# First batch's q and k in two token halves, constant products placed by the plan, and a plan that parts masks from two-input sums

## The chip, the cores and the metric

The kernel runs on one core of a Trainium2 chip. The metric is the device time of one execution in microseconds. The five engines are named as the profile names them: PE (TensorE; PEld are its weight loads), DVE (VectorE), ACT (ScalarE), POOL (GpSimd) and SP (SyncE). Each works through its own list of instructions in order and waits on semaphores for the others.

## What is computed

Attention with a few "beacon" keys in front, followed by a two-layer network. Cut to what matters (q, k and v are 8 batches x 8 heads x 576 tokens x 64, beacon_k and beacon_v have 16 tokens):

```python
k_all = np.concatenate([beacon_k, k], axis=2)          # 592 keys
v_all = np.concatenate([beacon_v, v], axis=2)
scores = scale * np.matmul(q, k_all.transpose(0, 1, 3, 2))
scores = np.where(causal, -1e9, scores)                # beacons are always seen
a = np.exp(scores - scores.max(-1, keepdims=True))
a /= a.sum(-1, keepdims=True) + 1e-09
x = np.matmul(a, v_all)  -> 4608 tokens x 512
h = x @ w_in                                            # 512 x 2048
g = h * (1.0 / (1.0 + np.exp(-1.702 * h)))
out = g @ w_out                                         # 2048 x 512
```

## The kernel before, in words

**Sets and chunks.** Four heads of one batch are a *set*: 128 partitions hold 4 heads x 32 rows. There are 16 sets, two per batch. For each set `e_load_qk` (L400) loads q and k by DMA from POOL's queue (288 KB each as f16, the DMA casts), `e_bk` (L442) casts the beacon keys on DVE and `e_turn` (L449) transposes k and q on DVE in 32x32 blocks (L451 for the beacons, L458 for the rest). A *chunk* is one stretch of score columns: `e_qk` (L477) makes the scores on PE (L491), `e_exp` (L499) takes the exponential on ACT (L502). Masks on the diagonal blocks follow on DVE (L516, a minimum of two inputs; in the first batch where the block lies among the first 288 tokens) or on POOL (L523). `e_av` (L571) multiplies the masked exponentials by ones (the row sums, "ones" in the profile) and by v (L582). DVE turns the sums, takes reciprocals (L592 to L603) and normalizes into xT (L616).

**The first batch.** Its sets 0 and 1 are taken in token halves: the first chunk of each set (qk0, qk1) covers tokens 0 to 287 alone, three more chunks cover the rest (qk2 to qk4 of set 0, qk5 to qk7 of set 1). Each needs the whole of q and k of its set, transposed. The scores of qk1 and qk2 are kept in four single banks of PSUM, those of the others in one large tile s, so that each of these others waits for the exponentials of the one before.

**The network.** Groups of tokens go through `m1` (PE, L640), an activation and `m2` (PE, L685). Later groups use products of fewer multiplications with sums taken by DVE (L705, L754, L770, L841). PSUM's four ring banks u0 to u3 are shared by `av`, `m1`, `m2` and the rest.

**The order.** `ORDER` at the top of the file lists, for each engine, the numbers of the operations in the order in which they are emitted; these lists were written out beforehand. `Plan.run` walks through the lists with a planned duration for each operation, so that every operation has a planned start. From that it does two things: it merges the five lists into one program order, and it gives every ring tile one of the banks, the one that the plan says is free earliest. Instructions of one engine always stand in the order of `ORDER`.

**DMA.** q, k, v, w_in and w_out go through POOL's queue, with at most 8 in flight: POOL waits at the ninth until the first has landed. The beacon keys go through the queues of SP and ACT (`load_bk`, L437), into a buffer that DVE has set to zero before (L305, L306, L1328). Stores of the output use SP.

**Constant products.** `FILL` (L314) names two places at which PE multiplies constants: 72 products of 112 columns ahead of qk0 and 2 products of 256 columns in f32 ahead of qk1 (L1358). No result uses them.

Of the kernel before, what the change touches and what calls it, by code (L numbers as in the profile page):

```python
# [7 lines left out]
F16 = mybir.dt.float16  # L8
# [9 lines left out]
        76, 100, 101, 102, 103, 111, 112, 119, 113, 114, 122, 126, 149, 131, 140, 152, 154, 129, 133, 136, 142, 163,  # L18
        166, 145, 169, 172, 175, 138, 156, 159, 161, 178, 184, 181, 199, 238, 202, 187, 205, 243, 208, 211, 217, 245,
        214, 193, 248, 188, 194, 269, 195, 196, 223, 274, 220, 224, 276, 189, 190, 252, 259, 279, 225, 229, 411, 230,  # L20
        231, 226, 414, 257, 283, 264, 262, 255, 290, 417, 288, 293, 295, 286, 232, 424, 301, 309, 331, 305, 303, 319,
        323, 315, 307, 311, 327, 325, 329, 313, 317, 321, 442, 433, 349, 350, 354, 351, 352, 355, 356, 445, 440, 436,
        438, 357, 360, 471, 370, 371, 361, 376, 377, 577, 365, 362, 363, 378, 366, 580, 481, 372, 367, 373, 368, 586,
        379, 486, 488, 484, 605, 382, 383, 496, 384, 607, 385, 490, 518, 610, 506, 494, 492, 520, 504, 516, 510, 500,
        512, 502, 514, 498, 508, 596, 543, 549, 538, 544, 545, 539, 540, 541, 738, 550, 565, 551, 546, 566, 741, 552,
        599, 603, 601, 619, 744, 554, 555, 556, 557, 624, 626, 622, 751, 559, 560, 561, 562, 567, 769, 634, 571, 572,
        568, 772, 760, 573, 574, 646, 658, 638, 648, 628, 650, 656, 798, 763, 765, 767, 630, 644, 642, 640, 636, 654,
        632, 652, 676, 681, 677, 682, 678, 683, 684, 904, 808, 703, 679, 704, 687, 907, 815, 811, 688, 705, 689, 913,
        692, 690, 697, 706, 698, 932, 699, 693, 694, 695, 700, 934, 813, 923, 709, 710, 711, 937, 712, 835, 817, 829,
        821, 837, 823, 839, 833, 819, 843, 825, 827, 831, 845, 847, 841, 1065, 930, 946, 865, 866, 892, 867, 893,  # L30
        868, 1068, 926, 928, 951, 949, 953, 1071, 894, 876, 877, 895, 878, 1078, 870, 871, 872, 873, 881, 1096, 882,
        883, 879, 884, 886, 1099, 887, 888, 889, 961, 1087, 1125, 898, 899, 900, 901, 967, 977, 957, 969, 959, 963,
        965, 973, 983, 975, 971, 979, 955, 981, 985, 1144, 1135, 1092, 1090, 1030, 1003, 1004, 1005, 1006, 1147,
        1138, 1142, 1140, 1094, 1153, 1008, 1009, 1024, 1014, 1025, 1172, 1010, 1015, 1031, 1011, 1032, 1174, 1026,
        1016, 1019, 1020, 1017, 1177, 1021, 1022, 1027, 1203, 1033, 1209, 1235, 1207, 1036, 1205, 1037, 1211, 1038,
        1212, 1039, 1219, 1215, 1251, 1239, 1163, 1186, 1237, 1241, 1221, 1243, 1223, 1244, 1225, 1247, 1227, 1228,
        1255, 1191, 1170, 1166, 1193, 1168, 1189, 1259, 1257, 1260, 1231, 1288, 1253, 1342, 1289, 1263, 1283, 1326,
        1346, 1284, 1348, 1285, 1344, 1286, 1290, 1350, 1330, 1351, 1294, 1304, 1354, 1295, 1328, 1335, 1358, 1305,
        1332, 1291, 1334, 1296, 1299, 1374, 1338, 1306, 1307, 1297, 1300, 1301, 1302, 1376, 1378, 1380, 1310, 1360,
        1362, 1311, 1312, 1364, 1382, 1383, 1316, 1313, 1367, 1366, 1317, 1386, 1318, 1319, 1449, 1370, 1406, 1407,  # L40
        1453, 1408, 1411, 1481, 1409, 1412, 1455, 1451, 1465, 1413, 1483, 1457, 1414, 1485, 1467, 1469, 1487, 1458,
        1417, 1461, 1427, 1490, 1489, 1418, 1428, 1419, 1420, 1429, 1474, 1471, 1473, 1497, 1422, 1493, 1423, 1430,
        1424, 1425, 1477, 1499, 1503, 1433, 1501, 1434, 1435, 1439, 1440, 1436, 1505, 1534, 1441, 1442, 1509, 1529,
        1530, 1531, 1506, 1540, 1532, 1541, 1535, 1550, 1551, 1536, 1537, 1542, 1545, 1552, 1546, 1547, 1543, 1548,
        1553, 1556, 1557, 1558, 1559, 1562, 1563, 1564, 1565,
    ],
    "ACT": [
        3, 1, 77, 79, 105, 106, 104, 107, 120, 115, 118, 123, 116, 117, 141, 143, 164, 167, 146, 170, 173, 176, 179,
        182, 185, 200, 239, 203, 206, 244, 209, 212, 246, 249, 215, 218, 270, 275, 197, 221, 277, 191, 280, 412, 227,
        415, 418, 233, 425, 427, 302, 310, 332, 320, 304, 306, 316, 308, 328, 326, 330, 312, 324, 314, 318, 322, 443,  # L50
        353, 446, 472, 475, 578, 581, 590, 587, 606, 608, 497, 491, 507, 519, 495, 521, 505, 493, 511, 501, 517, 513,
        503, 515, 499, 509, 611, 542, 739, 742, 745, 754, 752, 770, 773, 635, 647, 649, 629, 659, 651, 639, 657, 799,
        631, 643, 645, 641, 637, 655, 633, 653, 802, 905, 680, 908, 917, 914, 933, 935, 938, 836, 818, 822, 838, 840,
        830, 834, 820, 844, 828, 824, 832, 826, 846, 848, 842, 1066, 869, 1069, 1072, 1079, 1081, 1097, 1100, 1129,
        1126, 962, 968, 958, 978, 964, 966, 960, 970, 976, 974, 980, 972, 984, 956, 982, 986, 1145, 1007, 1148, 1154,
        1157, 1173, 1175, 1178, 1204, 1210, 1208, 1206, 1236, 1214, 1220, 1216, 1218, 1240, 1238, 1242, 1222, 1224,
        1252, 1250, 1226, 1246, 1248, 1230, 1234, 1256, 1258, 1232, 1254, 1343, 1264, 1266, 1262, 1327, 1347, 1345,
        1349, 1287, 1353, 1331, 1357, 1329, 1355, 1333, 1337, 1339, 1375, 1359, 1341, 1377, 1381, 1361, 1379, 1363,
        1365, 1389, 1387, 1385, 1369, 1450, 1371, 1454, 1373, 1482, 1410, 1452, 1456, 1466, 1484, 1460, 1468, 1486,
        1464, 1470, 1488, 1462, 1496, 1472, 1494, 1498, 1476, 1500, 1480, 1492, 1478, 1502, 1504, 1510, 1512, 1533,  # L60
        1508,
    ],
    "DVE": [
        75, 73, 74, 97, 98, 99, 82, 108, 78, 80, 81, 109, 110, 127, 128, 132, 150, 151, 155, 153, 130, 134, 135, 137,
        237, 87, 168, 235, 165, 171, 174, 139, 266, 157, 158, 162, 177, 160, 236, 180, 186, 183, 201, 204, 207, 408,
        210, 213, 267, 268, 92, 216, 219, 297, 409, 222, 410, 423, 253, 254, 260, 421, 261, 422, 298, 258, 284, 265,
        263, 256, 285, 291, 289, 292, 468, 296, 287, 294, 429, 299, 470, 300, 430, 469, 333, 431, 334, 345, 583, 432,
        337, 338, 346, 339, 434, 435, 341, 342, 335, 347, 348, 336, 441, 340, 437, 343, 439, 477, 358, 478, 584, 479,
# [39 lines left out]
    ],  # L108
}


class Op:
    __slots__ = (
        "eng", "dur", "deps", "pr", "due", "emit", "kind", "ring", "mode", "lat",
# [1275 lines left out]
```

## Time and profile before

| what | value |
|---|---|
| median of 3 runs | 326.31 us (325.89 to 327.42) |
| the profiled execution, its own time | 326.28 us |
| its span in the trace | 324.5 us |
| PE busy | 310.2 us, 96% of the span |
| DVE, ACT, POOL busy | 247.3, 220.3, 117.9 us |
| PE's granted clock, mean over the span | 0.987 |
| chain of waits: share of PE | 85% |

The profile page has the busy time of each engine, the span in 40 slices, the DMA queues, the chain of work that ended last and the costliest groups of instructions. A view by stretches gives the busy time of each engine and the clock that was granted to PE within a stretch of the span; the timeline lists instructions in order of time, neighbours of one kind merged: start, duration, engine, line, what it writes and reads, how many, and in brackets how long the engine had been idle and what ended that.

### The profile page before, as it was taken

The page shows a single profiled execution, that of the slowest core. Times are in us where ns is not written, and L with a number is a line of the kernel's source. Part 1 is how long each engine was busy: PE and PEld are TensorE (multiplying, and loading weights), DVE is VectorE, ACT ScalarE, POOL GpSimd, SP SyncE. Part 2 cuts the span into 40 slices and gives each one's busy share as a digit, 9 for nine tenths or more (in the row PEclk, how much of TensorE's full clock was granted, in tenths as well). Part 3 has the DMA queues.
Part 4 walks back from the last instruction along what each step waited for, and adds up shares of the span by engine and source line. Part 5 has one row for each costly group of instructions (what it writes and reads, how often), then busy time and mean ns, then how long its engine had stood idle before and what let it go on. Part 6 is the DMA issues. An engine that isn't in the chain of part 4 may idle for free.

```text
span 324.5 us, 10329 instructions
## 1 busy us (share of the span) xinstructions
PE 310.2 (96%) x4508; PEld 230.6 (71%) x4508; DVE 247.3 (76%) x481; ACT 220.3 (68%) x277; POOL 117.9 (36%) x178
## 2 busy tenths in 40 slices
PE   6499999999999999999999999999999999999995
PEld 6368755644786466755778878746887888888884
DVE  3678785984995879966979589977998884567584
ACT  1666877777776786679777686668768785675520
POOL 7585548385345605741257208510330000000000
PEclk9969999999999999999999999999999999999999
DMA  7999999989558911991069368510012000111113
GB/s 121 155 197 206 205 191 135 151 103 160 70 107 108 154 24 37 105 180 35 2 107 109 64 79 59 108 42 2 4 52 80 4 0 34 45 56 34 51 49 129
DMA packets 58222, 28.85 MB, mean 89 GB/s; under 512 B 41280, under 2 KB 53568, under 8 KB 58176
## 3 DMA queue, kind: packets, MB, share of 16 engines
q0 software_dynamic: 47552, 18.49, 49.3%
q1 hardware_dynamic: 10560, 9.69, 9.1%
q8 instruction: 35, 0.57, 0.7%
q14 instruction: 11, 0.09, 0.1%
q10 hardware_dynamic: 64, 0.01, 0.0%
HBM read 37.22 MB, written 9.44 MB: 144 GB/s over the span
## 4 chain that ended last, share of the span: by engine, by line
PE 85%; DMA 5%; ACT 3%; DVE 3%; POOL 2%; issue 1%; DVEq 0%; POOLq 0%
PE u L754 31%; PE u L640 24%; PE u L841 11%; PE u L582 9%; PE s L491 7%; DMA vb<-in_beacon_v_dram 3%; PE u L685 2%; DMA kn<-in_k_dram 2%; ACT E L502 1%; DVE osb L770 1%; DMA vb<-in_v_dram 1%; ACT L661 1%; DVE zs L541 1%; POOL E L523 1%; DVE tB L705 0%
## 5 line engine op out<-in xcount | busy, mean ns | idle before, releaser
L502 ACT ACTIVATE E<-s 128x2048 f16<-128x2048 f32 (+5 forms) x63 | 95.6, 1532 | 44.0 <-PE s L491 43.7
L523 POOL TENSOR_SCALAR_AFFINE_SELECT E<-E 128x512 f16<-128x512 f16 (+2 forms) x78 | 53.6, 706 | 95.8 <-ACT E L502 95.6
L640 PE MATMUL u<-xT,w 128*128 128x256 f16 (+1 forms) x512 | 86.8, 326 | 0.5 <-ACT g L661 0.4
L640 PEld LDWEIGHTS <-w 128*128 128x128 f16 x512 | 49.2, 98 | 32.8 <-issue 1.2
L754 PEld LDWEIGHTS <-g 128*128 128x128 f16 x512 | 48.7, 98 | 6.6 <-DVE g L705 0.2
L661 ACT ACTIVATE g<-u 128x512 f16<-128x512 f32 x80 | 43.4, 601 | 14.6 <-PE u L640 14.2
L754 PE MATMUL u<-w,g 128*128 128x256 f16 x384 | 50.4, 273 | 0.0
L770 DVE SCALAR_TENSOR_TENSOR osb<-u,osb 128x512 f32<-128x512 f32 x48 | 32.8, 684 | 16.8 <-PE u L754 15.5
L491 PEld LDWEIGHTS <-kT 32*128 32x128 f16 x1376 | 24.8, 94 | 22.4 <-issue 13.3
L754 PEld LDWEIGHTS <-sA 128*128 128x128 f16 x384 | 36.4, 98 | 5.2
L869 ACT ACTIVATE g<-u 128x512 f16<-128x512 f32 x48 | 27.3, 600 | 16.9 <-PE u L841 9.7
L491 PE MATMUL s<-qT,kT 32*128 32x32 f16 (+20 forms) x1328 | 33.7, 230 | 2.4 <-DVE kT L458 1.6
L754 PE MATMUL u<-tB,sA 128*128 128x256 f16 x256 | 35.1, 273 | 0.0
L418 POOL DMA_DIRECT2D vb<-in_v_dram x32 | 27.7, 870 | 18.5 <-PE u L582 15.5
L616 DVE TENSOR_TENSOR xT<-u,rz 128x352 f16<-128x352 f32 (+2 forms) x52 | 26.0, 519 | 7.5 <-PE u L582 6.8
L582 PE MATMUL u<-E,vb 128*32 128x288 f16 (+8 forms) x928 | 28.4, 269 | 2.0 <-DVE osb L770 1.0
L582 PEld LDWEIGHTS <-vb 128*32 128x32 f16 (+1 forms) x928 | 20.5, 99 | 7.9 <-issue 3.0
L458 DVE STREAM_TRANSPOSE qT<-qn 128x576 f32<-128x576 f32 x16 | 19.8, 1246 | 5.6 <-DMA qn<-in_q_dram 4.1
L541 DVE TENSOR_TENSOR zs<-zs,E 128x1344 f16<-128x1344 f16 (+2 forms) x36 | 23.1, 643 | 1.2 <-POOL E L523 0.5
L705 DVE TENSOR_TENSOR sA<-g 128x512 f16<-128x512 f16 x32 | 13.0, 417 | 13.3 <-ACT g L661 13.2
L458 DVE STREAM_TRANSPOSE kT<-kn 128x576 f32<-128x576 f32 x16 | 20.1, 1257 | 2.2 <-PE s L491 1.6
L841 PE MATMUL u<-xT,w 128*128 128x256 f16 x144 | 20.5, 273 | 0.0
(76 smaller groups left out, 394.5 us busy)
## 6 DMA issues: line engine op xcount, KB each, us to landing
out_dram<-osb SPq DMA_DIRECT2D x36, 256.0 KB, 2.7
qn<-in_q_dram POOLq DMA_DIRECT2D x16, 288.0 KB, 5.5
kn<-in_k_dram POOLq DMA_DIRECT2D x16, 288.0 KB, 5.7
vb<-in_v_dram POOLq DMA_DIRECT2D x24, 128.0 KB, 4.4
w<-in_moe_w_in_dram POOLq DMA_DIRECT2D x8, 256.0 KB, 7.6
w<-in_moe_w_out_dram POOLq DMA_DIRECT2D x4, 512.0 KB, 10.8
vb<-in_v_dram POOLq DMA_DIRECT2D x8, 112.0 KB, 4.2
vb<-in_v_dram POOLq DMA_DIRECT2D x8, 80.0 KB, 5.5
```

Of the source, the lines that this page charges most:

```text
L418: nc.gpsimd.dma_start(out=t[0 : hi - lo, j, h0:h1, :], in_=v[b, h0:h1, lo:hi, :].rearrange("h n d -> n h d"),)
L458: nc.vector.transpose(out=f32(dst.rearrange("p n e -> p (n e)")).rearrange("p (r t) -> p t r", t=TR), in_=f32(src[:, :]).rearrange("p (t c ...
L491: nc.tensor.matmul(ss[i][h][:, o : o + w], kT[s % NB2][r : r + 32, j * P : (j + 1) * P, d], qT[s % NB2][r : r + 32, a : a + w, d], start=( ...
L502: nc.scalar.activation(out=Es[s][:, :, c0:c1] if h is None else Es[s][:, h, c0:c1], in_=sall[i][:, :, o : o + c1 - c0] if h is None else s ...
L523: nc.gpsimd.affine_select(out=blk, in_=blk, compare_op=ALU.is_ge, fill=0.0, base=off + (Nb if j == 0 else 0), pattern=[[0, Q], [1, w]], ch ...
L582: nc.tensor.matmul(u[32 * h : 32 * h + 32, a:e], lhs, src[0:kw, h, col : col + e - a], start=first, stop=last, skip_group_check=s >= EARLY ...
L640: nc.tensor.matmul(u[:, o + a - t0 : o + e - t0], w1t[:, kp, nt * P : (nt + 1) * P], xT[:, kp, a % XR : (e - 1) % XR + 1], start=(kp == 0) ...
L661: nc.scalar.activation(out=gts[g][:, n0:n1, 0:w], in_=rings[("m1", g, n0)][:, 0 : n * w].rearrange("p (n w) -> p n w", n=n), func=AFT.Gelu ...
L754: nc.tensor.matmul(u[:, HM * mt : HM * (mt + 1)], lhs[:, n, mt * P : (mt + 1) * P], rhs[:, n, :], start=(n == 0 and mt == 0 and p not in ( ...
L770: nc.vector.scalar_tensor_tensor(out=osbs[(g, dst)][:, :], in0=rings[("p", g, p)][:, :], scalar=scale_of(g), in1=osbs[(g, src)][:, :], op0 ...
L841: nc.tensor.matmul(u[:, HM * n : HM * (n + 1)], lhs[x][:, (2 * i + n) * P : (2 * i + n + 1) * P], rhs[:, x, :], start=fresh and n == 0 and ...
L869: nc.scalar.activation(out=gts[g][:, n : n + 2, HM * h : HM * (h + 1)], in_=rings[src][:, :].rearrange("p (n w) -> p n w", n=2), func=AFT. ...
```

## The change

1. **Halves.** `load_qk`, `e_load_qk`, `turns` and `e_turn` take a `part`. For sets 0 and 1, q and k are loaded as two DMAs of 288 tokens each and transposed half by half. The first chunks (qk0, qk1) wait for the first halves alone. POOL issues the eight halves in the order q0a, k0a, k1a, k0b, q1a, q0b, k1b, q1b, where a is the first half. The key columns of the second half that a first chunk touches are set to zero beforehand.
2. **Beacon keys.** Those of sets 0 and 1 come in one round of four DMAs in place of two rounds of four. SP issues the other three rounds at its third to fourteenth places, and DVE sets their buffers to zero among the transposes of the first batch; before, the second of these rounds came at 25.47 us of the span and the third at 60.79 us.
3. **Constant products.** `FILL` goes. When the program is emitted, the gaps that the plan has on PE ahead of its time `WARM` are looked through, and where a ring bank is free in one, products of 256 columns in f16 are put in. That comes to 15 ahead of qk0, 11 ahead of qk1 and 2 ahead of the first m1.
4. **The plan.** In `Plan.run` a mask on POOL and a sum of two inputs on DVE do not overlap any more. This alters planned starts, and with them banks and the merged order.
5. **ORDER** is new. It differs from the old one in the first 57 of PE's 553 operations, 40 of ACT's 265, 51 of DVE's 433, 49 of POOL's 171 and 20 of SP's 54; behind them each list has the old operations in the old order. 447 ring operations get another bank.

In POOL's new list the loads behind the eight halves are: a v block, w_in, v, the constants for the masks, beacon_v, v, w_in, k of set 2, v, q of set 2, v, and then six w_in. In the old one they were w_in, q of set 2, three v, v, the constants, beacon_v, w_in, v and six w_in, with k of set 2 behind them. On PE, the second halves of sets 0 and 1 (av) come before the third m1 instead of after the fifth, and qk8 to qk10 come among the m1 of group 0.

```diff
@@ ORDER: all lists are new
...
+HELD = ("s", "zadd", "xsum", "wsum", "t", "mask")
...
+        o.port = 0
+        if eng == "POOL" and name.startswith("mask"):
+            o.port = 2
+        elif eng == "DVE" and name.rstrip("0123456789") in HELD:
+            o.port = 1
...
+                if o.port:
+                    t = max(t, held[3 - o.port])
...
+            held[o.port] = o.end
...
-    nc.vector.memset(bkf[:, 0:1, :], 0.0)
-    nc.vector.memset(bkf[:, 1:HS, :], 0.0)
+    nc.vector.memset(bkf[:, 0:HS, :], 0.0)
     for t in kT:
+        nc.vector.memset(t[:, Nb + HF : NKPAD // 5 * 3, :], 0.0)
...
-    FILL = {"qk0": ((72, 112, F16),), "qk1": ((2, 256, F32),)}
+    FIRST, WARM, COLS = 3800, 20000, 256
...
+        w = TR // 2 * D
+        nc.gpsimd.dma_start(
+            out=dst[:, w * part : w * (part + 1)],
+            in_=(q, k)[which][b, Q * hs : Q * hs + Q, HF * part : HF * (part + 1), :].rearrange(
+                "h (r t) d -> h r (t d)", t=TR // 2
+            ),
+        )
...
+        n, a, e = (TR, 0, S) if part is None else (TR // 2, HF * part, HF * (part + 1))
+        dst = kT[s % NB2][:, Nb + a : Nb + e, :] if which else qT[s % NB2][:, a:e, :]
+        src = (qn, kn)[which][s % NB3][:, a // 32 * D : e // 32 * D]
...
-            deps += [turn[(s, 0)], turn[(s, 1)]]
+            early = s < HS and c1 <= EHALF
+            deps += [turn[(s, 0, 0) if early else (s, 0)], turn[(s, 1, 0) if early else (s, 1)]]
...
-    load_bk(0, 1, (), ("SP", "ACT"))
-    load_bk(1, HS)
-    load_qk(0, 1)
-    load_qk(0, 0)
-    load_qk(1, 1)
-    load_qk(1, 0)
+    load_bk(0, HS, (), ("SP", "ACT"))
+    for part in range(2):
+        for s in range(HS):
+            for which in (1, 0):
+                load_qk(s, which, part=part)
...
-    idle = psu.tile([P, 512], F32, tag="u3", name="u3")
+    held, until = [None] * RING, FIRST
     for o in order:
-        for n, w, t in FILL.get(o.name, ()):
-            x = scrap.bitcast(t)
-            for _ in range(n):
-                nc.tensor.matmul(idle[:, 0:w], x[:, 0:P], x[:, 0:w], start=True, stop=True)
+        if o.eng == "PE" and o.start < WARM:
+            free = [(max([0] + [c.end for c in plan.closers.get(x, ())]), i) for i, x in enumerate(held)]
+            since, i = min(free)
+            n = int((2.0 if until > FIRST else 1.4) * (o.start - max(until, since + 200)) / COLS)
+            if n > 1:
+                idle = psu.tile([P, 512], F32, tag=f"u{i}", name=f"u{i}")
+                for _ in range(n):
+                    nc.tensor.matmul(idle[:, 0:COLS], scrap[:, 0:P], scrap[:, 0:COLS], start=True, stop=True)
+            until = o.end
+        if o.ring is not None and plan.tiles[o.ring] < RING:
+            held[plan.tiles[o.ring]] = o.ring
         o.emit()
```

## Prediction

> **What bounds the kernel now.** First the page: busy share in tenths, granted clock and DMA in 40 slices of 8.1 us.
>
> ```profile
> PE   6499999999999999999999999999999999999995
> ...
> PEclk9969999999999999999999999999999999999999
> DMA  7999999989558911991069368510012000111113
> ```
>
> PE is the bound from the third slice to the last; before that it is idle half the time, and in the third slice its clock is low, while DMA is full from the second slice to the eighth. What PE waits for from 23 us on (us in total, times, longest):
>
> ```profile
> PE u L582 <- DVE osb L770: 1.0, 2, 0.6
> PE u L841 <- DVE u L863: 0.6, 1, 0.6
> PE u L640 <- ACT g L661: 0.4, 1, 0.4
> PE u L582 <- issue: 0.3, 1, 0.3
> ```
>
> 2.3 us in 298. So behind the start only PE's own work counts, and whatever the start saves reaches the end; nothing behind it can give or take much. Then the start, by stretches (PE, PEld, DVE, ACT, POOL busy, clock, DMA):
>
> ```profile
> 8.96:12.37 3.41, 2.22 (x56) 1.63 (x60) 2.86 (x5) 1.94 (x2) 2.00 (x5) 1.00 1.05 134
> 12.37:15.79 3.42, 1.02 (x60) 0.81 (x51) 1.08 (x4) 3.25 (x5) 1.59 (x2) 1.00 2.05 162
> 15.79:19.20 3.41, 2.58 (x76) 1.86 (x78) 1.91 (x7) 3.14 (x6) 3.21 (x5) 0.50 1.72 182
> 19.20:22.61 3.41, 3.41 (x92) 2.59 (x88) 3.02 (x8) 1.45 (x1) 3.40 (x7) 0.50 1.28 204
> 22.61:26.03 3.42, 3.42 (x92) 2.80 (x81) 2.75 (x7) 2.54 (x4) 1.25 (x3) 1.00 1.24 205
> ```
>
> I chose these borders because the clock changes at 5.55, 15.79 and 22.61, a grid of 3.41 us. After 2.22 us of PE work in a stretch the clock stays, after 1.02 it halves; after 2.58 it stays at half, after 3.41 it is full again. The limits lie between these pairs. (The first 38 constant products start 93 ns apart, those after 5.55 us 49.) Last, the timeline:
>
> ```profile
> 18.42 0.62 PE L582 MATMUL u<-E,vb 128*32 128x288 f16 x12 [0.62 <-DMA vb<-in_beacon_v_dram]
> 18.97 0.83 PE L491 MATMUL s<-qT,kT 32*128 32x288 f16 x24
> 19.73 1.47 PE L582 MATMUL u<-E,vb 128*32 128x288 f16 x36
> ...
> 25.67 2.79 PE L640 MATMUL u<-xT,w 128*128 128x256 f16 x24
> 28.39 0.68 PE L582 MATMUL u<-E,vb 128*32 128x288 f16 x20
> ```
>
> PE runs without a gap from about 19 us, at half clock until 22.61.
>
> **The measure.** The changed PE list does the second halves (av) after two m1, not five. At 28.46 us the old kernel has done all that the new one has done when it starts its first second-half v product, and three m1 (2.73 us) and 20 v products (0.53 at full clock: 79 take 2.10) more. So the new kernel is level where that product starts at 28.46 - 2.73 - 0.53 = **25.2 us**; each us earlier is one us gained at the end.
>
> **The change part by part.**
>
> *Halves, first scores.* In the trace q0, k0, k1, q1 have landed at 6.09, 7.60, 9.10, 10.48: 1.5 us per load. A half is 0.75 by bytes: q0a at 5.35, k0a 6.1, k1a 6.85, q1a (fifth) 8.35. A half transpose is half of 1.25 us. So qk0 starts at 6.1 + 0.63 + 0.1 = 6.9, not 9.00. Four further transposes cost DVE nothing: it waited 2.8 us ahead of its masks. What a half costs no row shows. Bounds: 0.75, or 1.5 if a load costs the same whatever its size (6 us more for all eight). The nearest row is w_in, whose loads of 256 KB with rows of 1 KB land 1.28 us apart, the same rate; I take 0.75. POOL's four further issues (0.56 each) hide behind the queue, which has five or more loads in flight. I also bound the gain below nothing: if the slowest of 16 parts of q0 was late because of first accesses (first part 4.57, last 6.09), the half lands at up to 6.1 and qk0 gains 1.4.
>
> *ACT.* From exp0 on, ACT runs through: 1.94 for exp0, 3.41 from 12.54 to 15.95 for qk1's and one big one, 1.45 for the next. From 7.6 that ends at 14.4; qk5, which waits for it, ends by 15.2 (0.83 at half clock), 16.2 if the 11 constants ahead of qk1 run at half clock (2.35 us against 1.2) and hold qk1 up by a microsecond. The next wait is later, so this is covered.
>
> *v.* The next wait is the v block for the first half's products. In the old order beacon_v is the last of these, at 18.29. In the new one q of set 2 (1.5) and one v block (0.5) come behind: 16.3, and 16.4 with the beacon keys.
>
> *Beacon keys.* Two rounds (256 and 512 packets) move from 25.47 and 60.79 us into the full DMA stretch. When the 256 landed (29.7 to 32.6), two loads of 2.6 and 1.5 took 4.3: 0.2 us. So 0.6 for both; bounds 0, and 1.5 (768 packets of 31 ns on 16 engines). DVE's zeroing (0.27 and 0.49) falls where DVE waits; SP has no store until 51 us.
>
> *Second-half v and w_in.* The block that the first second-half product needs was issued at 13.67 and took 6.6: 20.27. Now k of set 2 is ahead (1.5), and the beacons (0.6): **22.4**. The last w_in moves from 27.98 to 30.1; its reader stands 7.9 us of work behind that product, so it is no earlier bound. w_out, one v block later, is read later than it lands.
>
> *PE from 16.4.* 36 products 1.47 at half clock, qk6 0.83, 12 products 0.49, 20 of ones 0.82: 20.0. Then two constants and m1 (10 x 213 ns at half clock, 109 at full), qk7 and the second m1. When does the clock rise? PE is then without a gap from 16.4, so a full stretch of the grid ends between 19.8 and 23.2; with the middle, 21.5: 7 of the 10 by then, 0.33 for the rest, 0.47 and 0.93 follow: **23.2**, after 22.4, so DMA does not hold it. 25.2 - 23.2 = 2.0; less 0.1 for waits between. With the rise at 23.2 it is 24.0 (gain 1.2), at 19.8 DMA sets 22.4 (gain 2.8).
>
> *Why half clock.* From 9.7 to 16.4 PE has qk3, ones, qk4, qk2, qk5, ones: about 2.6 us of work at full clock in 6.7, or 1.3 in a stretch, between 1.02 (fell) and 2.22 (stayed), nearer the first. The constants fill only the gaps ahead of qk0, qk1 and m1, not these.
>
> *The plan.* No operation is reordered behind the first 57 of PE's; masks and sums meet there as before. Only banks change: at best all 2.3 us of waits go, at worst as much comes, I estimate; I take 0, since every wait is short now.
>
> Sum: 326.28 (span 324.5 and 1.78 around it; the median 326.31 is the same) - 1.9 = **324.4**.
>
> **The rivals.**
> - *Full clock throughout.* If 1.3 us in a stretch is enough, PE reaches the product at 21.2 and waits for the v block at 22.4: gain 2.8, 323.5. For: 11 constants ahead of qk1. Against: the fall after 1.02.
> - *The clock rises late.* The 15 constants take 15 x 213 ns = 3.2 us, less than one stretch, where the 72 of before filled 2.14 to 5.55; so the clock may be low from the start, qk1's constants hold it up, and a gap in the run from 16.4 leaves the next stretch short as well: 3.41 us more at half cost 1.7, and 0.1 to 0.2 comes from each further wait. Gain 0.2: 326.1. [...]
> - *Slower: the queue.* If a half load costs much more than half, all loads behind shift, since DMA is full to the eighth slice. At 1.5 a half the v block lands at 28.4 and the product starts 3.2 late: 329.5. It decides from 2.8 us for all eight, 1.1 a half; the rows at 1.28 for 256 KB speak against it.
> - *It does not do what it says.* The parting of masks and sums, as above, moves no instruction; and constants in three gaps do not keep the clock.
>
> **Chances.** Forecast 0.48 (323.5 to 325.1 by itself; about 0.30 of it is faster by over 0.5%, that is under 324.68, since 0.5% is about what a measurement of this kernel can tell from no change). Full clock 0.20, faster. Late clock 0.20, within. Slow queue 0.06, slower. Banks or small waits that eat the gain 0.06, within. Faster 0.50, same 0.44, slower 0.06. Range 323.0 to 326.7: it leaves out the slow queue, and the ends where bank waits add to one of the others.
>
> **What would show it.** qk0 starting near 6.9; the first second-half product (L582's successor behind the second m1) near 23.2 with the v block landed before; half clock in some stretch between 12 and 23 us; the rest of the timeline shifted by a constant 2 us up to the end. Wrong would be: that product later than 25.2, PE waiting for v or w_in for over 1 us after it, or waits behind 60 us of much more or less than 2.3 us.

## The result, and the profile after

| what | before | after |
|---|---|---|
| median | 326.40 us (325.89 to 327.42, 4 runs) | 330.67 us (330.11 to 332.59, 4 runs) |
| the profiled execution, its own time | 326.28 us | 332.59 us |
| its span | 324.5 us | 330.8 us |

The ratio is 1.0137, with a 95% interval of 1.009 to 1.0185: slower. The predicted 324.4 us was wrong in sign, and its range (to 326.7) does not hold the result. The profiled execution is the slowest of the four; the spans of the other three are 328.3, 328.9 and 328.9 us.

First the page of the changed kernel: busy tenths, granted clock and DMA in 40 slices of 8.3 us.

```profile
PE   4679899999999999999999999999999999999995
...
PEclk9959799999999999999999999999999999999998
DMA  4999999859934950595046865640012000010113
```

Beside the rows of before: DMA has 4 tenths in its first slice, not 7, and is still at 9 in the eleventh, where before it had fallen to 5. The clock dips twice, in the third and the fifth slice. (Its record begins at 14.74 us; ahead of that the row shows 9, but the constants of 256 columns start 213 ns apart there, where the m1 products of 256 columns start 109 apart in the stretches at full clock and 213 in the one at half from 35.22 us, so I take it to have been at half.) Then what PE waits for up to 23 us:

```profile
PE s L514 <- DVE kT L474: 4.9, 1, 4.9
```

and from 23 us on:

```profile
PE s L514 <- issue: 1.8, 1, 1.8
PE u L605 <- DVE osb L793: 0.6, 1, 0.6
PE u L864 <- DVE u L886: 0.6, 1, 0.6
PE u L663 <- ACT g L684: 0.4, 1, 0.4
PE u L605 <- issue: 0.2, 1, 0.2
```

Three of these five rows are the old ones. New are two things: 4.9 us ahead of the first scores, and 1.8 us of "issue", idle time for which the profile knows no releaser. Before, the first of these was

```profile
PE s L491 <- DVE kT L458: 1.6, 1, 1.6
```

Where they are in the changed kernel, the timeline tells:

```profile
10.50 1.04 PE L514 MATMUL s<-qT,kT 32*128 32x288 f16 x24 [4.92 <-DVE kT L474]
...
27.91 0.43 PE L605 MATMUL u<-E,vb 128*32 128x288 f16 x7
...
32.66 0.30 PE L514 MATMUL s<-qT,kT 32*128 32x288 f16 x3
34.73 0.53 PE L514 MATMUL s<-qT,kT 32*128 32x288 f16 x21 [1.76 <-issue]
35.18 4.46 PE L663 MATMUL u<-xT,w 128*128 128x256 f16 x24
```

qk0 starts at 10.50 us (before 9.00, predicted 6.9). The first second-half v product is at 27.91, and 25.2 is level: **2.7 us late**. At 32.96 PE stops in the middle of a chunk of scores, after 3 of its 24 products, for **1.8 us**. Behind it 24 products of m1 take 4.46 us where they took 2.79: **1.7 us**, since the clock has halved. By stretches (PE, PEld, DVE, ACT, POOL, clock, DMA share, GB/s):

```profile
31.81:35.22 3.41, 1.65 (x33) 1.11 (x32) 2.35 (x5) 0.88 (x2) 3.15 (x5) 1.00 1.47 190
35.22:38.63 3.41, 3.41 (x19) 2.41 (x18) 0.00 (x0) 2.05 (x2) 3.34 (x6) 0.50 1.28 168
```

The gap leaves 1.65 us of work in one stretch, and the next is at half clock. 2.7 + 1.8 + 1.7 = 6.2 us, and the spans differ by 6.3. So there are two causes to find: late q and k, and a gap in which PE waits for nothing that is named. First the loads (up to 12 us: DMA share in 40 slices, then issues, KB each, median us from issue to landing):

```profile
DMA  0000000216324334902775788979999998999999
...
qn<-in_q_dram POOLq DMA_DIRECT2D x4, 144.0 KB, 8.6
kn<-in_k_dram POOLq DMA_DIRECT2D x4, 144.0 KB, 8.1
```

The same view of before (its q row holds a third load, of set 2):

```profile
DMA  0000000129599999999999999999999999989999
...
qn<-in_q_dram POOLq DMA_DIRECT2D x3, 288.0 KB, 7.4
kn<-in_k_dram POOLq DMA_DIRECT2D x2, 288.0 KB, 6.1
```

Loads of half the size take longer than whole ones did (8.6 and 8.1 us against 7.4 and 6.1), and the DMA engines, full from 3.3 us before, are far from full until 6 us. Each of these loads has sixteen completions in the trace, as many as the profile counts DMA engines. Sorted, in us:

```
before q0   4.57 4.58 4.63 4.68 4.75 4.76 4.81 4.82 4.94 5.20 5.23 5.29 5.76 5.78 5.91 6.09
after  q0a  3.30 3.35 3.38 3.39 3.40 3.41 3.44 3.47 3.48 3.55 3.58 3.60 7.28 7.29 7.33 7.34
after  k0a  4.04 4.07 4.11 4.11 4.12 4.15 4.24 4.26 7.50 7.52 7.53 7.56 9.23 9.29 9.32 9.66
after  k1a  4.76 4.80 4.84 4.86 7.74 7.80 7.80 7.87 9.50 9.54 9.57 9.86 10.71 10.72 10.72 10.73
```

Of q0a twelve parts are done at once and four take until 7.3; of k0a eight are done at once, four when q0a's four are through, four at 9.2 to 9.7; of k1a four each. I read this as loads that put their rows on **four engines each**, the next load on the next four, while twelve engines have no row of it. By this reading 128 rows are 32 per engine, and at 107 ns (the median packet of 1152 B) I estimate 3.4 us; q0a's last four completions come 3.7 us after the other twelve. (The trace doesn't name the engine of a packet; between 3.0 and 4.5 us it has 2 to 6 packets of 1152 B under way at a time.) The source of a half is 4 heads x 32 rows, and between the heads lies the other half; of a whole load it was 128 evenly spaced rows. That the number four comes from the four heads is a guess of mine that this trace does not show; runs 6, 10, 11 and 12 are about it.

### The profile page after: what moved, and what is told of

It reads as the page before. It is cut to its first block, busy times and chain, and to the rows that moved or that the text cites. A ratio compares the mean times of both kernels' runs of the same rounds, so it can differ in the third digit from the quotient of the medians.

```text
span 330.8 us, 10232 instructions
## 1 busy us (share of the span) xinstructions
PE 312.8 (95%) x4460; PEld 230.3 (70%) x4460; DVE 247.8 (75%) x486; ACT 220.7 (67%) x277; POOL 121.4 (37%) x182
## 4 chain that ended last, share of the span: by engine, by line
PE 84%; DMA 7%; DVE 4%; ACT 2%; issue 1%; POOL 0%; DVEq 0%; POOLq 0%
PE u L777 30%; PE u L663 24%; PE u L864 11%; PE u L605 8%; PE s L514 7%; PE u L708 3%; DMA vb<-in_v_dram 2%; DMA kn<-in_k_dram 2%; DMA w<-in_moe_w_in_dram 2%; ACT E L525 1%; DVE osb L793 1%; ACT L684 1%; DVE zs L564 1%; DVE qT L481 0%; DVE kT L481 0%
## 5 line engine op out<-in xcount | busy, mean ns | idle before, releaser
L663 PE MATMUL u<-xT,w 128*128 128x256 f16 (+1 forms) x512 | 88.3, 331 | 0.6 <-ACT g L684 0.4
L663 PEld LDWEIGHTS <-w 128*128 128x128 f16 x512 | 50.1, 99 | 33.6 <-issue 1.4
L793 DVE SCALAR_TENSOR_TENSOR osb<-u,osb 128x512 f32<-128x512 f32 x48 | 32.8, 684 | 16.4 <-PE u L777 15.5
L514 PEld LDWEIGHTS <-kT 32*128 32x128 f16 x1376 | 25.9, 95 | 26.2 <-issue 14.2
L514 PE MATMUL s<-qT,kT 32*128 32x32 f16 (+20 forms) x1328 | 34.4, 232 | 8.6 <-DVE kT L474 4.9
L481 DVE STREAM_TRANSPOSE qT<-qn 128x576 f32<-128x576 f32 (+1 forms) x18 | 20.0, 1118 | 6.9 <-DMA qn<-in_q_dram 3.6
L564 DVE TENSOR_TENSOR zs<-zs,E 128x1344 f16<-128x1344 f16 (+2 forms) x36 | 23.1, 644 | 1.2 <-POOL E L546 0.5
L481 DVE STREAM_TRANSPOSE kT<-kn 128x576 f32<-128x576 f32 (+1 forms) x18 | 20.4, 1133 | 4.6 <-DMA kn<-in_k_dram 2.4
```

The costliest lines, as they stand in the source:

```text
L481: nc.vector.transpose(out=f32(dst.rearrange("p n e -> p (n e)")).rearrange("p (r t) -> p t r", t=n), in_=f32(src).rearrange("p (t c) -> p ...
L514: nc.tensor.matmul(ss[i][h][:, o : o + w], kT[s % NB2][r : r + 32, j * P : (j + 1) * P, d], qT[s % NB2][r : r + 32, a : a + w, d], start=( ...
L663: nc.tensor.matmul(u[:, o + a - t0 : o + e - t0], w1t[:, kp, nt * P : (nt + 1) * P], xT[:, kp, a % XR : (e - 1) % XR + 1], start=(kp == 0) ...
L793: nc.vector.scalar_tensor_tensor(out=osbs[(g, dst)][:, :], in0=rings[("p", g, p)][:, :], scalar=scale_of(g), in1=osbs[(g, src)][:, :], op0 ...
```

## The experiments

Theory: **half loads on 4 of 16 DMA engines** make all that follows late. Rivals: the constants and the clock; the queue's order; the plan's banks; the rows' size. Later a second theory for the gap is added: **instruction blocks**. Medians of before, run beside them, are 325.9 to 326.1 us throughout.

**1. Whole loads in the changed kernel.**

```diff
-        if part is None:
+        if part == 1:
+            return
+        if part in (None, 0):
```

> The changed kernel, but q and k of sets 0 and 1 are loaded by four whole loads (4 x 32 rows of 1152 numbers, in the order q0, k0, k1, q1), as in the kernel before; the transposes by halves, the orders, the constants and the plan are kept. Theory (a half load has its 128 packets on only 4 of the 16 DMA engines, so q0a and k0a land at 7.34 and 9.66 us and all that is behind them shifts): q0 lands near 6.1, k0 near 7.6, q1 near 10.5, each with 16 parts of much the same time; qk0 starts near 8.4 instead of 10.50, the first second-half v product comes at 24 to 26 instead of 27.91, and the time is 324.5 to 328 us, 3 to 6 below the changed kernel's 330.7. Rival (constants and clock: 15 + 11 + 2 constants do not keep the clock as the 72 + 2 did): loads land early, but half clock behind 11 us as before, product at 27 or later, time 329 to 331. Rival (order of the queue: k of set 2 and the beacon keys ahead of v): v and w_in land late all the same, PE waits for them, time 328 to 330.

Measured 327.44 us (326.93 to 329.3), 1.0055 of before (1.003 to 1.008), so 3.2 us below the changed kernel. k0 lands at 7.02, qk0 starts at 7.86. Its timeline:

```profile
25.08 1.18 PE L607 MATMUL u<-E,vb 128*32 128x288 f16 x40
...
29.34 0.30 PE L516 MATMUL s<-qT,kT 32*128 32x288 f16 x3
30.91 0.53 PE L516 MATMUL s<-qT,kT 32*128 32x288 f16 x21 [1.27 <-issue]
```

The loads are a cause: the product stands at 25.08, level with before. The gap stays, after the same three products, though the program runs 3 us earlier, and is as large as what is left over before. The clock is low from 16.16 to 22.98 us, much as before (15.79 to 22.61), and from 9.33 to 12.74 as well, where before it was full.

**2. Half loads in the kernel before.**

```diff
-        nc.gpsimd.dma_start(out=dst[:, :], in_=rows_of((q, k)[which], s))
+        if s >= HS:
+            nc.gpsimd.dma_start(out=dst[:, :], in_=rows_of((q, k)[which], s))
+            return
+        w = TR // 2 * D
+        for part in range(2):
+            nc.gpsimd.dma_start(
+                out=dst[:, w * part : w * (part + 1)],
+                in_=(q, k)[which][0, Q * s : Q * s + Q, HF * part : HF * (part + 1), :].rearrange(
+                    "h (r t) d -> h r (t d)", t=TR // 2
+                ),
+            )
```

> The kernel before, but q and k of sets 0 and 1 are each loaded as two half loads, one behind the other, and transposed in two halves of the same operation; first chunks still wait for the whole of q and k, orders, constants and plan are those of before. Theory (4 of 16 DMA engines per half): parts of q0's first half land at 7 us or later, k0 whole at 10 to 12 instead of 7.60, q1 at 14 to 15 instead of 10.48, qk0 at 11 to 13 instead of 9.00; time 2 to 5 us over before, 328.5 to 331.5. Rivals by which the loads are not the cause (constants and clock, or the order of the queue): q1 lands within 1 us of before, qk0 within 0.5 of 9.00, and the time is 326 to 327.

Measured 329.41 us (328.94 to 330.28), 1.0108 (1.0084 to 1.0131). q0's first half lands at 7.39, k0 whole at 11.69, q1 at 15.11, and qk0 starts at 11.46: other than was expected, it does not wait for the second half of k0, only for the first (10.62) and its turn. Put into the kernel before, with the transposes cut in two, the loads cost 3.3 us; taken alone out of the changed one, they give 3.2.

**3. The constants of before in the changed kernel.**

```diff
-    FIRST, WARM, COLS = 3800, 20000, 256
...
+    FILL = {"qk0": ((72, 112, F16),), "qk1": ((2, 256, F32),)}
```

> The changed kernel with the constants of the kernel before: 72 products of 112 columns ahead of qk0 and 2 of 256 columns in f32 ahead of qk1, in place of 15, 11 and 2 placed by the plan. Theory (half loads on 4 of 16 DMA engines): q0a and k0a land at 7.3 and 9.7 as in the changed kernel, qk0 at 10.5, product at 27 to 28, time 329 to 331; up to 1.8 less than that only if the stall at 33 us, an instruction fetch, does not recur with the other program. Rival (constants and clock): the 72 products raise the clock to full near 5.6 and hold it until qk0, the 11 constants and the chunks behind run at full clock, product at 25 to 26, time 326 to 328.

Measured 329.17 us (329.08 to 329.79), 1.0101 (1.0084 to 1.0118). Loads (q0a 8.02, k0a 9.87), qk0 (10.71) and product (27.09) are within 0.9 us of the changed kernel's, and the clock falls at 11.0 and 17.82 again: not the rival's picture. Most of the 1.5 us that it gained lie in the gap: "issue" is 0.7 us in two pieces, not 2.0. The exchange puts in 48 more constants in all. The one effect of it that the rows show so far behind is that all later instructions stand further on in PE's list.

**4. Without the parting in the plan.**

```diff
-                if o.port:
-                    t = max(t, held[3 - o.port])
```

> The changed kernel without the parting of masks and two-input sums in the plan; only planned starts differ, and with them banks and merged order. Theory (half loads): nothing in the first 16 us changes, time within 0.7 of the changed kernel's 330.7. Rival (the new banks cost waits behind 30 us): 1 us or more below it.

Measured 330.45 us (329.88 to 332.57), 1.0148 (1.0112 to 1.0185): the parting costs nothing that these runs could tell (0.2 us, with intervals of over 1 us to either side). Its profiled execution has a span of 328.1, near the other three of the changed kernel, and no late half clock: product at 26.78, and from 23 us on

```profile
PE s L512 <- issue: 1.5, 1, 1.5
...
PE u L603 <- issue: 0.5, 1, 0.5
```

**The second theory.** PE's matmuls and weight loads, counted along the list in each trace, have their gaps at the same numbers in all kernels: 705 and 961 (both in after and in run 4; 961 in runs 1 and 3; 705 in run 2). 961 - 705 = 256. And the trace has packets of 16 KB in a queue of kind "instruction", 35 of them for PE's 8,920 matmuls and weight loads (by the page of the changed kernel), one per 256. I read this as PE getting its instructions in blocks of 256, one packet for each. In us, the packet after number 705 and PE at the next border:

```
            number 705   next packet        PE reaches 961   goes on
before        23.06       26.51 to 27.40        29.40         29.40
after         28.52       32.18 to 33.21        32.66         34.72
run 1         25.21       28.44 to 29.33        29.35         30.91
run 4         27.75       31.38 to 32.33        31.89         33.67
```

Up to 35 us the packet starts, in nearly all rows of all runs, 2.0 to 4.3 us after PE has begun the block before, and takes 0.9 to 1.0. Where PE had to wait by 0.2 us or more, it went on 1.3 to 1.7 us after the packet's end, and no block in any trace began sooner than 1.3 us after its packet. Every row of "issue" that PE has from 20 us on, in all fifteen traces, stands at such a border. Ahead of 45 us these next blocks began 5.0 to 6.5 us after the one before. The kernel before has such a wait too, its "issue: 0.3": it stands at 65.23 us, one number short of 2241 (705 and six times 256), after a block of 3.6 us, 1.3 us behind its packet. Ahead of 45 us before needed 5.65 and 6.34 us for its two densest blocks, and just had no gap; the new order has the second halves of both sets (v products 29 ns apart) with scores between and behind them (24 in 0.5 us), 256 instructions in 4.14 us. What sets a packet off, the runs do not show; the border's number, the packets and the times are measured.

**5. Whole loads and the constants of before** (the edits of 1 and 3).

> The changed kernel with whole loads of q and k of sets 0 and 1 (as in the run with whole loads, 327.44 us) and, besides, the constants of the kernel before (72 and 2 in place of 15, 11 and 2). These shift PE's instruction list by 96 places. Theory of the blocks: PE fetches its instructions in blocks of 256 (one packet of 16 KB each), a new block is ready 5 to 6.4 us after PE has begun the one before it, and the gap of 1.3 us at 30 us of the whole loads, 1.8 in the changed kernel, comes where PE does 256 instructions in 4.1 us; with the shift the densest block takes 4.5, so the gap is 0.5 to 1.0 and the time 326.3 to 327.2. Theory that the clock is what is left: the 72 products keep it full through the first chunks, the first second-half product comes by 24, time 325 to 326. If neither: 327.4.

Measured 326.78 us (326.2 to 328.93), 1.0022 (1.0003 to 1.0042). Gap 0.81 at 961 after a block of 4.23 us (4.5 was expected), product at 24.83: the theory of the blocks, and inside its range. The clock was full from 5.93 to 16.17, much as before, and still the product is not at 24: what remains is not the clock ahead of 16 us.

**6. Each half load as four loads of one head.**

```diff
+        for h in range(Q):
             nc.gpsimd.dma_start(
-                out=dst[:, w * part : w * (part + 1)],
+                out=dst[32 * h : 32 * h + 32, w * part : w * (part + 1)],
```

> The changed kernel with each half load split by head, four loads of 32 rows of 1152 B in place of one of 4 x 32 rows. Theory (the number of DMA engines goes by the slowest dimension, 4 heads; 32 rows give all 16): the parts of each load land within 1 us of one another, q0a is whole near 1 us after its last issue plus the 2.3 us that a load takes from issue, that is by 6 to 6.5; but POOL issues 32 loads at 0.55 us each, so k0a is issued by 5.8 and whole near 8 to 8.5, qk0 starts near 9, and the last half lands at 19 to 21 instead of 15.21; v and w_in come later still, time 329 to 333. Rival (the rows of 1152 B or the first accesses to memory are slow by themselves): parts of q0a still land at 7 us or later while others of the same load are there at 3.5.

Measured 334.95 us (334.64 to 335.29), 1.0267 (1.023 to 1.0304), slower than expected. The parts of q0a's first load land from 3.34 to 3.89, all sixteen together; q0a is whole at 5.03 and k0a at 6.98, sooner than expected. So rows of 1152 B are not slow. But POOL's 32 issues at half a microsecond hold up all that follows: PE waits 3.8 us for q1's turn and 4.5 us for a mask.

**7. The changed kernel with its list shifted.** `range(n)` products of 256 columns become `range({"qk0": 80, "qk1": 20}.get(o.name, 4 * n))` of 64.

> The changed kernel with more and smaller constants: 80, 20 and 8 products of 64 columns ahead of qk0, qk1 and the first m1, in place of 15, 11 and 2 of 256. PE is idle there anyway; what changes is that all later instructions stand some 160 places further on in PE's list. Theory of the blocks (as above): no border falls behind 256 instructions that take less than 5.3 us, so the gaps without a wait between 25 and 40 us (0.5 and 1.8 us in the changed kernel) go, and the time falls to 328 to 329.3. Rival (the gap belongs to that place of the program, a wait that the profile doesn't name, or the clock): a gap of 1.5 us or more stays at the fourth product of the same chunk, and the time at 330 to 331.

Measured 331.09 us (330.79 to 331.43), 1.0152 (1.0121 to 1.0184): a miss. The operation ahead of which the second lot stands isn't called qk1, so 44 were put there, not 20, and the list moved by 208 places, not 160. PE's waits from 23 us on:

```profile
PE u L663 <- issue: 1.7, 1, 1.7
PE u L605 <- issue: 1.0, 1, 1.0
```

The gaps are not at the fourth product of that chunk any more, which is against the rival; they are again at 961 and now at 1217, after blocks of 5.20 and 4.21 us. The theory's place holds, the time expected from it does not, because the shift was a bad one.

**8. Whole loads with a shifted list** (the edit of 7 with 60 for 80; again 44 in the middle, 168 places as said).

> Whole loads of q and k of sets 0 and 1 (the run of 327.44 us) with 60, 30 and 8 products of 64 columns in place of 15, 11 and 2 of 256: PE's list is shifted by 168 places. Theory of the blocks: the gap of 1.3 us at 30 us goes, and the time is 325.5 to 326.6, level with the kernel before (326.1), since the first second-half product at 25.1 stands where the kernel before has it (25.2). Rival (gap not from the blocks): 327 to 328.

Measured 327.15 us (326.2 to 328.1), 1.0033 (1.0014 to 1.0051): inside the rival's range. Gaps of 0.32 and 0.77 are left at 705 and 961 in place of 1.56, after blocks of 5.40 and 5.15. The profiled execution, at 326.20 the fastest of ten, has before's span, 324.5, as the theory has it; what makes the median 1 us longer no trace shows.

**9. Run 5 with one m1 put between** the dense operations.

```diff
-        174, 146, 144, 246, 164, 167, 169, 177, 251,
+        174, 146, 144, 177, 246, 164, 167, 169, 251,
```

> The run with whole loads and the constants of the kernel before (326.78 us), with one m1 of PE's list (the third, m1.0.4) moved ahead from behind the second halves of set 1 to between those of set 0 and the next scores. Theory of the blocks: 8 slower products within the block that took 4.23 us and ended in a gap of 0.8 raise it to about 4.9, so the gap falls to 0.3 or less, and the time to 326.0 to 326.5. Rival (the gap is not a matter of how dense PE's list is there): gap and time stay, 326.6 to 327.0.

Measured 326.61 us (325.87 to 326.99, 12 runs), 1.0008 (0.9993 to 1.0023): level with before, and by 0.01 us in the rival's range. The block takes 5.59 us and its gap is gone, without a further shift (0.4 us of "issue" is left at 65.64, the border at 2241). That fits the theory, by which it counts how long the block takes. But 0.74 us of the 5.59 are a wait, since the moved m1 came too early for its input; without it the block would take 4.85, less than the 5.0 us after which a next one began at the earliest. So the run does not show what the slower products alone would give:

```profile
26.25 1.03 PE L665 MATMUL u<-xT,w 128*128 128x256 f16 x8 [0.74 <-DVE xT L641]
```

**10. Whole loads in before, with heads as a dimension of their own.**

```diff
+            src = (q, k)[which][b, Q * hs : Q * hs + Q].rearrange("h (r t) d -> h r (t d)", t=TR)
```

> The kernel before, with the same four whole loads of q and k of sets 0 and 1 (128 rows of 2304 B each), only written with the heads as a dimension of their own (4 x 32 rows instead of 128 rows). Bytes, packets, issues and order are those of before. Theory (the slowest dimension, 4, sets the number of DMA engines): the 32 rows of an engine take 32 x 192 ns = 6.1 us, so q0 and k0 land at 9.5 to 10.5 instead of 6.09 and 7.60, qk0 starts at 11 to 12 instead of 9.00, and the time is 1.5 to 3 us over before. Rival (half loads are slow for their size, their rows of 1152 B or their number): lands as before, time 326.

Measured 326.38 us (325.67 to 328.08), 1.0013 (0.9994 to 1.0033). q0's sixteen parts land from 4.71 to 5.88: the theory's numbers failed. 4 x 32 evenly spaced rows went like 128 rows, so the run says nothing for either side on the loads. By chance it shows the blocks in the old order: the clock was low for one stretch, not two, PE did a block in 4.41 us, and stood at its border:

```profile
22.86 0.36 PE L495 MATMUL s<-qT,kT 32*128 32x160 f16 x13 [0.95 <-issue]
```

**11. The same with every other head**, so that the spacing is uneven (the first batch's result is another one).

```diff
+            src = (q, k)[which][0].rearrange("(h x) (r t) d -> x h r (t d)", x=HS, t=TR)[s]
```

> In the run before this one the four heads of a set lie one behind the other in memory, so its 4 x 32 rows are 128 evenly spaced rows again, and it tested nothing. Here, in the kernel before, set 0 of the first batch takes q and k of heads 0, 2, 4, 6 and set 1 of heads 1, 3, 5, 7 (v and the rest as before, so the first batch's result is another one); the four loads have the 128 rows of 2304 B of before, but the heads are no longer evenly spaced with the rows. Theory (4 heads are the slowest dimension, so 4 DMA engines per load): 32 rows x 192 ns = 6.1 us on each of four engines, q0 whole at 9 to 10 instead of 6.09, k0 at 10 to 11 instead of 7.60, qk0 at 11 to 12.5 instead of 9.00, time 328 to 329.5. Rival (half loads are slow for the length or number of their rows): lands as before, time 326 to 326.5.

Measured 331.79 us (331.09 to 332.07), 1.0184 (1.016 to 1.0207). Twelve parts of q0 land by 3.77 and four at 11.47 to 12.16; k0 is whole at 13.17, later than expected, as a packet took 252 ns in the mean, not 192.

```profile
PE s L494 <- DVE kT L461: 6.5, 1, 6.5
```

Same bytes, rows, packet size and number of loads as before: only the spacing of the heads differs, and it costs 5.9 us. The rival on size and number falls.

**12. Half loads of even rows in the changed kernel** (9 of every 18 tokens; the first batch's result is another one).

```diff
-            in_=(q, k)[which][b, Q * hs : Q * hs + Q, HF * part : HF * (part + 1), :].rearrange(
-                "h (r t) d -> h r (t d)", t=TR // 2),
+            in_=rows_of((q, k)[which], s)[:, w * part : w * (part + 1)],
```

> The changed kernel, but a half load takes the first (or last) 1152 B of each of the 128 rows that a whole load has, that is 9 of every 18 tokens in place of the first 288: as many bytes, packets and issues as the half loads of the change, but 128 evenly spaced rows. The tokens of q and k stand in another order, so the first batch's result is another one. Theory: all 16 DMA engines, so q0a lands at 5.0 to 5.9, k0a at 6.1 to 6.8, qk0 starts at 7 to 7.6 (the prediction had 6.9), the first second-half v product comes at 23.2 to 24.5, and the time is 324 to 325 plus the gap of a block border at about 30 us (1.3 to 2), that is 325.3 to 327. Rival (half loads land late for another reason, the size of their packets or the issues): q0a and k0a as late as in the changed kernel, time 329 to 331.

Measured 325.95 us (325.38 to 327.25, 10 runs), 1.0005 (0.9988 to 1.0021). Loads (up to 12 us, as above) and timeline:

```profile
DMA  0000000117989999999899999999999999999999
...
qn<-in_q_dram POOLq DMA_DIRECT2D x4, 144.0 KB, 5.3
kn<-in_k_dram POOLq DMA_DIRECT2D x4, 144.0 KB, 4.8
```

```profile
6.38 0.64 PE L512 MATMUL s<-qT,kT 32*128 32x288 f16 x24 [0.80 <-DVE kT L472]
...
23.03 0.43 PE L603 MATMUL u<-E,vb 128*32 128x288 f16 x7
...
29.56 0.52 PE L512 MATMUL s<-qT,kT 32*128 32x288 f16 x21 [1.49 <-issue]
```

k0a is there at 5.54, and the product at 23.03, where 23.2 was predicted. The half loads of uneven rows cost 330.67 - 325.95 = 4.7 us (4.3 by the ratios to before). But the 2.2 us of gain at the product are mostly taken by the gaps (1.5 and 0.2 of "issue"): level with before.

**13. Run 12 with its list shifted by 168 places** (the edit of 8).

> The run before this one (half loads of 128 even rows, so with the first batch's tokens in another order and its result another one; 325.95 us) with 60, 44 and 8 constants of 64 columns in place of 15, 11 and 2 of 256, which moves PE's list on by 168 places. Theory (two causes make up the whole difference from the prediction: half loads on 4 DMA engines, and gaps at borders of 256 instructions): with the borders moved, the gaps at 23.6 and 29.6 us (0.46 and 1.78) fall to 0.5 or less together, the first second-half product stays near 23.1, and the time is 324.0 to 324.8, the predicted 324.4. Rival (something else holds the rest, and the gap only stands in its place): the gap goes, but waits of as much come, 325.5 to 326.3.

Measured 325.28 us (324.19 to 326.5, 12 runs), 0.9968 (0.9951 to 0.9986): below before, and between theory and rival. The gap at 30 us is gone. But the product, expected near 23.1, comes at 25.25, since in the profiled execution another block border has come ahead of it:

```profile
20.11 0.22 PE L603 MATMUL u<-E,vb 128*32 128x48 f16 x1 [0.78 <-issue]
...
25.25 1.18 PE L603 MATMUL u<-E,vb 128*32 128x288 f16 x40
```

Block 705 began 6.4 us after 449; the gap left 2.64 us of work in the stretch from 17.14, and the clock, low there, rose one stretch later, at 23.98. So a gap may cost more than itself. Whether all of the remaining 0.9 us to the predicted 324.4 is made of such gaps stays open: the twelve spans are 322.5 to 324.8, and only this one has a trace.

A ledger of the profiled executions that share the new order of PE (run 9 moves an m1), in us against before. "Late" is the first second-half product less 25.2; "issue" is that idle time from 23 us on, less the 0.3 of before.

| kernel | late | issue | else | sum | span less 324.5 |
|---|---|---|---|---|---|
| after | 2.7 | 1.7 | 1.7 half clock | 6.1 | 6.3 |
| 1 whole loads | -0.1 | 1.0 | | 0.9 | 0.7 |
| 3 old constants | 1.9 | 0.4 | 0.5 kT | 2.8 | 3.0 |
| 4 no parting | 1.6 | 1.7 | | 3.3 | 3.6 |
| 5 whole loads, old constants | -0.4 | 0.6 | | 0.2 | 0.6 |
| 6 by head | 7.4 | 0.6 | 0.6 vb | 8.6 | 9.0 |
| 7 shifted | 2.6 | 2.4 | | 5.0 | 5.1 |
| 8 whole loads, shifted | -0.2 | 0.2 | | 0.0 | 0.0 |
| 12 even half rows | -2.2 | 1.4 | | -0.8 | -0.6 |
| 13 even half rows, shifted | 0.1 | -0.3 | | -0.2 | -0.7 |

## Why the prediction was wrong, point by point

- **"A half is 0.75 by bytes"**, the step that failed and gave the wrong sign. A half load lay, by its completions, on four of sixteen engines: of q0a twelve came by 3.60 us and the last four from 7.28. q0a landed at 7.34 (5.35 predicted), k0a at 9.66 (6.1), the last half at 15.21 (10.6 by its sum); with even rows (run 12) they land at 4.62, 5.54 and 11.01, 0.91 apart. The upper bound, 1.5 "if a load costs the same whatever its size", did not hold for these first landings, though from one half to the next it was 1.12, and "the rows at 1.28 for 256 KB" were those of loads whose rows are evenly spaced. The nearest rival was the one on the queue, with a chance of 0.06 and 329.5 us, but its path was another: it had the v block late behind full DMA engines, and what came was 4.9 us of wait ahead of qk0, half empty engines until 6 us and no wait for v. That its 3.2 us are near the measured 2.7 is luck.
- **The chain from the landing to the product** was right: with even half rows qk0 starts at 6.38 (6.9) and the product at 23.03 (23.2), but in part by luck. The first-half v products begin at 16.26 (16.4), yet PE waits for no v block: the last wait ahead of them is one for ACT (0.52 us, at 15.07), which was said to be covered. The clock, low from 13.15, is full again at 19.98 (21.5), for which the prediction's own sum gives 22.5; but from 20.17 to the product PE took 2.86 us, and the sum at full clock has 2.49. No wait for the beacon keys shows.
- **The level point**, 25.2 us, holds: see the ledger, whose sums come within 0.5 us.
- **"So behind the start only PE's own work counts, and whatever the start saves reaches the end"** failed too, by most of the gain. The row "issue: 0.3" was in the quoted waits, and not asked about; it is a wait at a border of 256 instructions. Moving the second halves ahead puts 256 short instructions together, and at that time PE got no more than 256 in 5.0 to 6.5 us. The sum has no term for this; it was 1.4 us in the run that had the rest as predicted.
- **The plan and its banks**, taken at 0: right as far as the runs can tell (run 4, 0.2 us; the named waits from 23 us on are 1.6 us after and 2.0 before).
- **The clock.** Half clock was forecast until 21.5; it lasted to 24.98 in the changed kernel, since all came later. The rivals on it were not needed: with the constants of before the loads were as late, and the product 0.8 us earlier (run 3). But "the limits lie between these pairs" does not hold as a limit on busy time: see the last section.
- **"It does not do what it says"**: right for the parting. The constants did not keep the clock either. With the late loads nor did those of before (run 3, low from 11.0); with whole loads those of before did, from 5.93 to 16.17 (run 5), and the new ones did not (run 1, low from 9.33 to 12.74).
- **What would show it** did so: a product later than 25.2.

## What to carry to other kernels

Before a load is cut into pieces, look whether its rows are still evenly spaced over all outer dimensions: here a half of 4 x 32 rows with a gap behind every 32 landed at 7.34 us (q0a, four of its sixteen completions 3.7 us behind the rest), the whole at 6.09, and a half of 128 even rows at 4.62 (run 12). Count the instructions of PE in blocks of 256: where short products make a block shorter than the next one takes to come (5.0 to 6.5 us here ahead of 45 us, some 3.6 at 65), work that was moved forward waited at the border (1.76 us in the changed kernel, 1.49 in run 12). Longer products between them should help; only run 9 tried it, and not cleanly. An idle row without a releaser is a question to be answered, even at 0.3 us.

## What the runs showed of the hardware

- The place where PE waited for instructions went with the number in its list (705, 961, 1217), not with the program: 48 constants more, ahead of everything, went with 1.5 us less (run 3). At 50 to 63 us the instruction packet starts 0.2 to 0.6 us after PE has begun the block before, in the traces of the changed kernel and of run 12; ahead of 40 us it was 2.0 to 4.3. In the changed kernel all DMA moves 196 to 210 GB/s from 40 to 50 us and 93 to 183 from 50 to 65, so full queues are a likely reason for the late packets; it is not shown, and in runs 7 and 9 a packet at 58 us came 2.8 and 3.0 us after it as well.
- PE's busy time in a stretch of 3.41 us, as the traces give it, does not decide the clock of the next one. At full clock, 1.65 us (after) and 1.98 (run 4, from 13.14) were followed by half clock, and 1.76 (run 6, from 6.20) and 1.97 (run 4, from 30.21) by full. At half clock, 2.64 (run 13) and 2.95 (run 2, from 11.05) did not raise it, 2.83 (run 4, from 9.73) and 3.25 (after) did. What else counts, the runs do not show.
- A load of uneven rows, of whose completions some came late, brought 384 packets of 4 bytes more than one of even rows. POOL's queue has sixteen of them for each load before (1,472 for 92) and in run 12 (1,536 for 96), but 4,608 in the changed kernel, with eight loads of uneven rows, and 3,008 in run 11, with four. 384 is 12 times 32, as if, by the reading of four engines, each engine without a row had one for each of the 32 rows of the others. What they are, no run here shows.
